# Attention scores from two-part rounded operands, and one reduction for the maxima of two heads

## The chip, the cores and the metric

The kernel runs on one core of a Trainium2 chip. The metric is the device time of one execution in microseconds (us); lower is better. The engines are TensorE (PE for its matmuls, PEld for its weight loads), VectorE (DVE), ScalarE (ACT), GpSimd (POOL) and SyncE (SP, which only issues transfers).

## The reference

Attention over 4 batches, 12 heads, 448 positions and 64 values for each head, then two feed-forward layers of 768 to 2048 to 768 on the 1792 rows that result:

```python
q_n, k_n = rmsnorm(q, g_q), rmsnorm(k, g_k)        # x / sqrt(mean(x*x) + 1e-6) * g
scores = scale * q_n @ k_n.T                       # (448, 448) for each head
attn = exp(scores - scores.max(-1)); attn /= attn.sum(-1) + 1e-9
x = attn @ v                                       # rows of 12 heads * 64 = 768
h = x @ w_in;  x = (s * relu(h)**2 + b) @ w_out    # layer 1
h = x @ w_in2; x = (h * cos(h)) @ w_out2           # layer 2
```

q, k, v and x are float32. The weights come as float64 and are turned to float32 on the chip.

## The kernel before, in words

**Attention.** Two heads make a pair; there are 24 pairs, worked on one after the other, each in four chunks of 112 query rows: 96 chunks `s`, where pair `i = s // 4` and `r = s % 4`. Heads 0 and 1 of a pair lie in partitions 0 to 63 and 64 to 127 of the transposed q and k (`qT`, `kT`), so that their score matmuls use different row halves of TensorE's array. One chunk is `scores(s)` (line 203): two float32 matmuls, one for each head, into two PSUM banks; two reductions on DVE for the maxima (line 222); two exponentials on ACT with the sums beside them (line 230). Two chunks later `turn` (line 240) transposes the exponentials, four transposes for each head into a bank tagged "tp" (two such banks), and copies them out, head 0 by ACT (line 254), head 1 by DVE (line 252). `mix` (line 264) multiplies them with v.

q and k of pair i+1 are made ready during pair i: `flip` (line 186) transposes them on PE at r = 1 (q) and r = 2 (k); `unflip` (line 194) copies the result to SBUF, q by ACT (line 199), k by DVE with the gains multiplied in (line 201). Squares (line 145 on POOL, 147 on ACT) and their sums (line 153, DVE) come three pairs ahead, and `norms` two.

**What sets the order.** The loop at line 313 emits each step. At r = 1 that is: flip q, scores, unflip q, turn; at r = 2: flip k, scores, unflip k, turn, mix. The helper `line` (line 118) ties each attention instruction to the one emitted before it on the same engine: on PE always, on ACT and DVE until 36 chunks (9 pairs, `ALONE`) have been emitted. Within those the engines take the attention's instructions in just the order of the code. Engines work through their queues in order. What isn't tied (the weights' preparation, and after 36 chunks all of ACT's and DVE's work) stands where the program's scheduler put it when the kernel was built. `follow` makes the score matmuls of chunk s wait for the exponentials of chunk s-2.

**Feed-forward.** The first 9 pairs run alone, with some preparation of weights beside them. Then the units of the feed-forward layers are mixed in: `unit_in` (18 matmuls of 448 columns, line 437) and `unit_out` (line 489 in layer 1, 516 in layer 2). Their float32 operands are split into a rounded high part and the low rest (`float32r`, which PE takes in one pass), and each product is three matmuls: high by high, low by high, high by low (`products`, line 100). How many attention steps go between two units is worked out from costs written by hand (0.93 for the scores of a chunk, `PAIR` = 12.1 for a pair). Each half of a weight tile passes ACT (lines 408, 409), DVE (412 to 414), ACT (371) and POOL (374).

Of the kernel before, what the change touches and what calls it, by code (L numbers as in the profile page):

```python
# [10 lines left out]
F32 = mybir.dt.float32  # L11
F32R = mybir.dt.float32r
# [3 lines left out]
ALU = mybir.AluOpType  # L16
# [17 lines left out]
def body(ctx, tc, q, k, v, g_q, g_k, w1_in, w1_out, s_in, b_in, w2_in, w2_out, out):  # L34
# [16 lines left out]
    LAG_T = 2  # L51
    START, GATE = 4, 10
    ALONE = 9
    PAIR = 12.1
    LOOK = 8

    const = ctx.enter_context(tc.tile_pool(name="const", bufs=1))
# [42 lines left out]
    def products(w, x):  # L100
        return ((w[0], x[0]), (w[1], x[0]), (w[0], x[1]))
# [9 lines left out]
    def attention(keep):  # L111
# [6 lines left out]
        def line(engine, first, last=None):  # L118
            if engine in tail and (engine == "PE" or len(exps) <= NCH * ALONE):
                issue_after(first, tail[engine])  # L120
            tail[engine] = last or first
            return first

        def load(i, what):
            b, hp = pairs[i]
            for nm in what:
                src = {"q": q, "k": k, "v": v}[nm]
                t = att.tile([CP, 2, NCH, D], F32, tag=f"raw{nm}", name=f"raw{nm}_{b}_{hp}")
                st[i][nm] = t
                src = src[b, 2 * hp:2 * hp + 2]  # L130
                if i == 0 and nm == "q":
                    t = t.rearrange("p h c d -> p (h c d)").rearrange("p (c h d) -> p c h d", c=NCH, h=2)
                    for j in range(2):
                        nc.sync.dma_start(t[:, :, j, :], src[j].rearrange("(p c) d -> p c d", c=NCH))
                    st[i]["q by chunk"] = t
                else:
                    nc.sync.dma_start(t, src.rearrange("h (p c) d -> p h c d", c=NCH))

        def squares(i):
            b, hp = pairs[i]  # L140
            for nm in "qk":
                t = st[i]["n" + nm] = att.tile([CP, NCH, 2, D], F32, tag=f"n{nm}", name=f"n{nm}_{b}_{hp}")
                t, src = t.rearrange("p c h d -> p (c h d)"), st[i][nm].rearrange("p h c d -> p (h c d)")
                if 1 < i <= ALONE + 2:
                    nc.gpsimd.tensor_tensor(t, src, src, ALU.mult)
                else:
                    line("ACT", nc.scalar.activation(t, src, AF.Square))

        def means(i):
            b, hp = pairs[i]  # L150
            ss = att.tile([CP, 2, 8], F32, tag="ss", name=f"ss_{b}_{hp}")
            for n, nm in enumerate("qk"):
                line("DVE", nc.vector.reduce_sum(ss[:, n, :], st[i]["n" + nm].rearrange("p c h d -> p (c h d)").rearrange("p (a d) -> p a d", d=D), axis=AX.X))  # L153
            tiny = nc.vector if i == 0 else nc.gpsimd
            m = st[i]["m"] = att.tile([CP, 16], F32, tag="m", name=f"m_{b}_{hp}")
            tiny.tensor_scalar(m, ss.rearrange("p a b -> p (a b)"), 1.0 / D, 1e-6, ALU.mult, ALU.add)

        def norms(i):
            b, hp = pairs[i]
            m, tiny = st[i]["m"], nc.vector if i == 0 else nc.gpsimd  # L160
            ln = att.tile([CP, 16], F32, tag="ln", name=f"ln_{b}_{hp}")
            line("ACT", nc.scalar.activation(ln, m, AF.Ln))
            y = att.tile([CP, 16], F32, tag="y", name=f"y_{b}_{hp}")
            line("ACT", nc.scalar.activation(y, ln, AF.Exp, scale=-0.5))
            z = att.tile([CP, 16], F32, tag="z", name=f"z_{b}_{hp}")
            kept = (lambda z: line("DVE", z)) if i == 0 else lambda z: z
            kept(tiny.tensor_tensor(z, y, y, ALU.mult))
            kept(tiny.tensor_tensor(z, z, m, ALU.mult))
            kept(tiny.tensor_scalar(z, z, -0.5, 1.5, ALU.mult, ALU.add))
            kept(tiny.tensor_tensor(y, y, z, ALU.mult))  # L170
            rs = y.rearrange("p (a h c) -> p a h c", a=2, h=2)
            if i == 0:
                st[i]["rs"] = y[:, 0:2 * NCH]
            for n, nm in enumerate("qk"):
                if i == 0 and n == 0:
                    continue
                kept(tiny.tensor_tensor(
                    st[i]["n" + nm].rearrange("p c h d -> p h c d"), st[i][nm],
                    rs[:, n].unsqueeze(3).to_broadcast([CP, 2, NCH, D]), ALU.mult))

        def bank(i, name):
# [12 lines left out]
        def unflip(i, nm):  # L194
            b, hp = pairs[i]
            pt = st[i]["p" + nm]
            t = st[i][nm + "T"] = att.tile([P, S], F32, tag=f"{nm}T", name=f"{nm}T_{b}_{hp}")
            if nm == "q":
                line("ACT", nc.scalar.copy(t, pt))
            else:  # L200
                line("DVE", nc.vector.tensor_scalar(t, pt, gqk, None, ALU.mult))

        def scores(s):
            i, c = divmod(s, NCH)
            key = f"{pairs[i][0]}_{pairs[i][1]}_{c}"
            sc = [ps.tile([P, 512], F32, tag="sc", name=f"sc_{key}_{j}", bufs=4)[:CP, :S] for j in range(2)]
            mm = []
            for j in range(2):
                half = slice(j * D, (j + 1) * D)
                mm.append(nc.tensor.matmul(sc[j], st[i]["qT"][half, c * CP:(c + 1) * CP], st[i]["kT"][half, :], start=True, stop=True))  # L210
            line("PE", *mm)
            issue_after(mm[1], mm[0])
            if s > 1:
                follow(mm[0], exps[s - 2])
            if s == START:
                marks["start"] = mm[1]
            if c == 0:
                st[i]["sums"] = att.tile([CP, NCH, 2], F32, tag="sums", name=f"sums_{key}", bufs=3)
                st[i]["top"] = att.tile([CP, 8], F32, tag="top", name=f"top_{key}", bufs=3)
            tops = [st[i]["top"][:, 2 * c + j:2 * c + j + 1] for j in range(2)]  # L220
            for j in range(2):
                line("DVE", nc.vector.tensor_reduce(tops[j], sc[j], axis=AX.X, op=ALU.max, negate=True))  # L222
            scale = [1.0, 1.0]
            if i == 0:
                both = st[i]["top"][:, 2 * c:2 * c + 2]
                line("DVE", nc.vector.tensor_tensor(both, both, st[i]["rs"][:, 2 * c:2 * c + 2], ALU.mult))
                scale = [st[i]["rs"][:, 2 * c + j:2 * c + j + 1] for j in range(2)]
            for j in range(2):
                pr = st[i]["pr", j, c] = att.tile([CP, S], F32, tag="pr", name=f"pr_{key}_{j}", bufs=8)
                e = line("ACT", nc.scalar.activation(pr, sc[j], AF.Exp, bias=tops[j], scale=scale[j], accum_out=st[i]["sums"][:, c, j:j + 1]))  # L230
            exps.append(e)

# [80 lines left out]
        for s in range(n + 5):  # L313
# [10 lines left out]
                cost += 0.46  # L324
            if s < n:
                scores(s)
                cost += 0.93
            if r == 1:
                emit(unflip, i + 1, "q")
            if r == 2:  # L330
# [96 lines left out]
    def unit_in(layer, seg, ck, f, b):  # L427
# [18 lines left out]
        if layer == 0:  # L446
            r = ma.tile([P, S], F32, tag="t0", name=f"r_{key}")
            nc.scalar.activation(r, h, AF.Relu)
            r2 = ma.tile([P, S], F32, tag="t1", name=f"r2_{key}")
            nc.gpsimd.tensor_tensor(r2, r, r, ALU.mult)  # L450
            gt = ma.tile([P, S], F32, tag="t2", name=f"gt_{key}")
            nc.vector.tensor_scalar(gt, r2, sb[:, 0:1], sb[:, 1:2], ALU.mult, ALU.add)  # L452
        else:
            hs = ma.tile([P, S], F32, tag="t0", name=f"hs_{key}")
            nc.scalar.copy(hs, h)
            h = hs
            kk = ma.tile([P, S], F32, tag="t1", name=f"kk_{key}")
# [229 lines left out]
```

## Time and profile before

| | us |
|---|---|
| three timed runs | 1299.21, 1291.16, 1298.42 |
| median of the runs | 1298.42 |
| the profiled execution | 1293.51 |
| its span, first to last instruction | 1291.4 |

The granted TensorE clock of the profiled execution was 0.996 of full speed. In the rows below, a duration is that of one instruction from its start to its end, and neighbours on an engine overlap at the ends; how long an instruction keeps its engine is read from the start of the next one. In a timeline, "x4" stands for four instructions merged in one row, and the number in brackets is idle time before the row with what ended it.

### The profile page before, as it was taken

To read this page: it belongs to the slowest core of one execution; us is meant where nothing else is said; L and a number is where in the kernel's file an instruction comes from. 1 tells how busy PE (TensorE), PEld (TensorE's weight loads), DVE (VectorE), ACT (ScalarE), POOL (GpSimd) and SP (SyncE) were. 2 spreads that over 40 slices of the span, in tenths; PEclk is the share of its full clock that TensorE was granted. 3 is DMA by queue.
4 is the path that set the end of the run, shared out by engine and by line. 5 is a ranking of instruction groups with operands and counts; after the bars stand their busy time and mean duration, and the time that the engine had idled before them with its cause. 6 is when DMAs were issued, how large, how long until landed. Compare 5 with 4: busy or idle time off the path is not lost.

```text
span 1291.4 us, 18598 instructions
## 1 busy us (share of the span) xinstructions
PE 1246.4 (97%) x6624; PEld 1034.9 (80%) x6624; DVE 857.9 (66%) x1456; ACT 744.8 (58%) x1674; POOL 581.5 (45%) x643
## 2 busy tenths in 40 slices
PE   5999998999999999989999999999999999999998
PEld 2555675677677767779999999999999999999998
DVE  5898768876868767654454456854767767677655
ACT  4787767755666555525332225787656656566640
POOL 3665646454553524414333233565444445354531
PEclk9999999999999999999999999999999999999999
DMA  3333324543344223353222112111212111111105
GB/s 97 108 99 120 99 90 126 159 127 102 123 133 126 100 89 94 106 165 104 78 71 69 55 56 74 51 49 51 71 50 74 50 50 49 49 50 50 62 1 171
DMA packets 82222, 111.32 MB, mean 86 GB/s; under 512 B 8113, under 2 KB 72145, under 8 KB 82129
## 3 DMA queue, kind: packets, MB, share of 16 engines
q1 hardware_dynamic: 82128, 110.13, 27.8%
q8 instruction: 52, 0.85, 0.3%
q14 instruction: 42, 0.34, 0.1%
HBM read 86.51 MB, written 23.59 MB: 85 GB/s over the span
## 4 chain that ended last, share of the span: by engine, by line
PE 58%; DVE 18%; ACT 14%; POOL 4%; issue 3%; DMA 3%; SPq 0%; DVEq 0%; ACTq 0%; POOLq 0%
PE ph L437 24%; PE po L516 14%; PE po L489 13%; ACT pr L230 4%; DVE t L413 3%; DVE t L414 3%; DVE top L222 2%; PE sc L210 2%; PE av L271 2%; PE tp L248 2%; DVE c L412 2%; DVE gt L461 2%; DVE ss L153 1%; DVE gt L462 1%; ACT pT L254 1%
## 5 line engine op out<-in xcount | busy, mean ns | idle before, releaser
L437 PE MATMUL ph<-xh,wl 128*128 128x448 f32 x768 | 283.4, 369 | 0.0
L437 PE MATMUL ph<-xl,wh 128*128 128x448 f32 x768 | 281.6, 367 | 0.0
L437 PE MATMUL ph<-xh,wh 128*128 128x448 f32 x768 | 280.0, 369 | 0.0
L467 POOL TENSOR_TENSOR gl<-gt,gh 128x448 fp32r<-128x448 f32 x128 | 157.0, 1231 | 185.0 <-ACT gh L466 184.9
L374 POOL TENSOR_TENSOR wl<-t,wh 128x384 fp32r<-128x384 f32 x128 | 139.1, 1102 | 71.7 <-ACT wh L371 70.7
L437 PEld LDWEIGHTS ph<-xh,wh 128*128 128x128 f32 x768 | 144.1, 188 | 16.5 <-issue 2.0
L489 PE MATMUL po<-gh,wh 128*128 128x448 f32 x384 | 145.9, 382 | 11.2 <-DVE acc L498 10.6
L498 DVE TENSOR_TENSOR acc<-po,acc 128x448 f32<-128x448 f32 x168 | 103.2, 619 | 80.3 <-PE po L489 80.1
L230 ACT ACTIVATE pr<-sc,top 112x448 f32<-112x448 f32 x184 | 116.4, 635 | 67.1 <-DVE top L222 66.9
L371 ACT CAST wh<-t 128x384 fp32r<-128x384 f32 x200 | 95.4, 513 | 103.4 <-PE po L489 53.3
L516 PE MATMUL po<-wh,gh 128*128 128x384 f32 x448 | 152.1, 340 | 2.3 <-ACT acc L522 1.1
L437 PEld LDWEIGHTS ph<-xh,wl 128*128 128x128 f32 x768 | 144.3, 188 | 12.1 <-issue 2.0
L437 PEld LDWEIGHTS ph<-xl,wh 128*128 128x128 f32 x768 | 144.3, 188 | 12.1 <-issue 1.3
L516 PE MATMUL po<-wl,gh 128*128 128x384 f32 x448 | 149.8, 335 | 0.4 <-POOL wl L374 0.4
L516 PE MATMUL po<-wh,gl 128*128 128x384 f32 x448 | 149.8, 334 | 0.0
L524 DVE TENSOR_TENSOR acc<-po,acc 128x384 f32<-128x384 f32 x196 | 105.4, 551 | 60.3 <-PE po L516 60.2
L489 PE MATMUL po<-gl,wh 128*128 128x448 f32 x384 | 142.2, 371 | 0.0
L489 PE MATMUL po<-gh,wl 128*128 128x448 f32 x384 | 142.1, 370 | 0.0
L465 POOL TENSOR_TENSOR gt<-hs,gt 128x448 f32<-128x448 f32 x64 | 78.3, 1223 | 129.0 <-ACT gt L464 118.7
L222 DVE TENSOR_REDUCE top<-sc 112x1 f32<-112x448 f32 x192 | 112.9, 616 | 23.2 <-PE sc L210 22.9
L466 ACT CAST gh<-gt 128x448 fp32r<-128x448 f32 x128 | 71.3, 564 | 97.9 <-DVE gt L452 59.6
L248 PEld LDWEIGHTS tp<-ident,pr 112*112 112x112 f32 x768 | 78.6, 133 | 60.5 <-issue 12.5
(89 smaller groups left out, 2258.4 us busy)
## 6 DMA issues: line engine op xcount, KB each, us to landing
raw<-in_moe_w_in_dram SPq DMA_DIRECT2D x64, 384.0 KB, 3.4
raw<-in_moe_w_out_dram SPq DMA_DIRECT2D x64, 384.0 KB, 3.2
t<-wd SPq DMA_DIRECT2D x72, 192.0 KB, 2.4
wd<-t SPq DMA_DIRECT2D x64, 192.0 KB, 3.1
rawk<-in_k_dram SPq DMA_DIRECT2D x24, 224.0 KB, 3.5
rawv<-in_v_dram SPq DMA_DIRECT2D x24, 224.0 KB, 3.0
rawq<-in_q_dram SPq DMA_DIRECT2D x23, 224.0 KB, 3.1
xd<-xf SPq DMA_DIRECT2D x12, 224.0 KB, 3.9
```

Source lines behind the costliest of these rows:

```text
L222: line("DVE", nc.vector.tensor_reduce(tops[j], sc[j], axis=AX.X, op=ALU.max, negate=True))
L230: e = line("ACT", nc.scalar.activation(pr, sc[j], AF.Exp, bias=tops[j], scale=scale[j], accum_out=st[i]["sums"][:, c, j:j + 1]))
L248: mm = [nc.tensor.transpose(tp[:, kc * CP:(kc + 1) * CP], pr[:, kc * CP:(kc + 1) * CP], ident[:CP, :CP]) for kc in range(NCH)]
L371: z = nc.scalar.copy(wh, w)
L374: eng.tensor_tensor(wl, w, wh.bitcast(F32), ALU.subtract)
L437: nc.tensor.matmul(h, a, m, start=(c == 0 and n == 0), stop=(c == NE - 1 and n == 2))
L465: nc.gpsimd.tensor_tensor(gt, h, gt, ALU.mult)
L467: nc.gpsimd.tensor_tensor(gl, gt, gh.bitcast(F32), ALU.subtract)
L489: marks["out"] = nc.tensor.matmul(po, a, m, start=(f == 0 and n == 0), stop=(f == CF - 1 and n == 2))
L498: nc.vector.tensor_tensor(at, po, at, ALU.add)
L516: nc.tensor.matmul(po, a, m, start=(f == 0 and n == 0), stop=(f == CF - 1 and n == 2))
L524: nc.vector.tensor_tensor(at, po, at, ALU.add)
```

## The change

The score operands are split as in the feed-forward layers, and each chunk's two matmuls become six, head by head in turn, into one tile of two banks. The two maxima of a chunk come from one reduction over both banks. q and k of a pair lie in one tile, so that their squares and sums are one instruction each (two for pair 0). To find room, the exponentials get 7 buffers in place of 8, and layer 1's squared activation is written in place while attention runs. The hand-written costs follow.

```diff
-    PAIR = 12.1
+    PAIR = 11.0
...
         def unflip(i, nm):
             pt = st[i]["p" + nm]
-            t = st[i][nm + "T"] = att.tile([P, S], F32, tag=f"{nm}T", name=f"{nm}T_{b}_{hp}")
+            hi, lo = (att.tile([P, S], F32R, tag=f"{nm}{z}", name=f"{nm}{z}_{b}_{hp}") for z in "hl")
+            st[i][nm + "T"] = hi, lo
             if nm == "q":
-                line("ACT", nc.scalar.copy(t, pt))
+                line("ACT", nc.scalar.copy(hi, pt))
+                line("DVE", nc.vector.tensor_tensor(lo, pt, hi.bitcast(F32), ALU.subtract))
             else:
-                line("DVE", nc.vector.tensor_scalar(t, pt, gqk, None, ALU.mult))
+                line("ACT", nc.scalar.activation(hi, pt, AF.Copy, scale=gqk))
+                line("DVE", nc.vector.scalar_tensor_tensor(lo, pt, gqk, hi.bitcast(F32), ALU.mult, ALU.subtract))
 
         def scores(s):
-            sc = [ps.tile([P, 512], F32, tag="sc", name=f"sc_{key}_{j}", bufs=4)[:CP, :S] for j in range(2)]
+            both = ps.tile([P, 2, 512], F32, tag="sc", name=f"sc_{key}", bufs=2)[:CP, :, :S]
+            sc = [both[:, j, :] for j in range(2)]
             mm = []
-            for j in range(2):
-                half = slice(j * D, (j + 1) * D)
-                mm.append(nc.tensor.matmul(sc[j], st[i]["qT"][half, c * CP:(c + 1) * CP], st[i]["kT"][half, :], start=True, stop=True))
+            for n, (x, y) in enumerate(products(st[i]["qT"], st[i]["kT"])):
+                for j in range(2):
+                    half = slice(j * D, (j + 1) * D)
+                    mm.append(nc.tensor.matmul(sc[j], x[half, c * CP:(c + 1) * CP], y[half, :], start=(n == 0), stop=(n == 2)))
...
-            for j in range(2):
-                line("DVE", nc.vector.tensor_reduce(tops[j], sc[j], axis=AX.X, op=ALU.max, negate=True))
+            line("DVE", nc.vector.tensor_reduce(st[i]["top"][:, 2 * c:2 * c + 2], both, axis=AX.X, op=ALU.max, negate=True))
...
-                cost += 0.93
+                cost += 0.65
...
-            r2 = ma.tile([P, S], F32, tag="t1", name=f"r2_{key}")
+            r2 = pools["mb"].tile([P, S], F32, tag="t1", name=f"r2_{key}") if "mb" in pools else r
```

## Rows read from the trace of the kernel before

**Rows 1.** The page: busy time, share of the span and instructions of each engine.

```profile
PE 1246.4 (97%) x6624; PEld 1034.9 (80%) x6624; DVE 857.9 (66%) x1456; ACT 744.8 (58%) x1674; POOL 581.5 (45%) x643
```

**Rows 2.** Busy by stretch: length; PE, PEld, DVE, ACT, POOL; clock; DMA share; GB/s.

```profile
50.00:100.00 50.00, 48.88 (x313) 25.73 (x311) 44.88 (x82) 39.38 (x112) 31.67 (x52) 1.00 0.34 105
100.00:140.00 40.00, 38.91 (x244) 19.75 (x242) 35.49 (x66) 32.63 (x93) 23.73 (x42) 1.00 0.38 121
140.00:525.00 385.00, 369.82 (x2016) 268.78 (x2016) 279.27 (x489) 241.15 (x590) 182.38 (x223) 0.99 0.36 113
```

**Rows 3.** The chain of waits, 95 to 125 us: shares by line; start, us, what.

```profile
by line: ACT pr L230 29.9%; DVE top L222 12.8%; ACT pT L254 11.4%; DVE c L412 11.3%; DVE ss L153 7.9%; DVE t L413 5.6%; ACT c L408 4.7%; ACT qT L199 4.2%; DVE pT L252 3.5%; DVE t L414 3.1%; ACT xh L96 3.0%; issue 0.8%; ACT ln L162 0.8%; ACT
...
94.96 0.42 ACT qT L199
...
98.01 1.13 DVE c L412
...
99.22 0.56 DVE t L413
...
101.84 1.19 DVE ss L153 x2
...
103.64 1.34 ACT pr L230 x4
...
107.31 0.42 ACT qT L199
...
119.67 0.42 ACT qT L199
```

**Rows 4.** Timeline of PE, three places alone and one at 411 us.

```profile
104.17 1.01 PE L210 MATMUL sc<-kT,qT 64*112 64x448 f32 x4
105.11 0.98 PE L248 MATMUL tp<-ident,pr 112*112 112x112 f32 x8
...
108.75 1.72 PE L271 MATMUL av<-pT,rawv 112*64 112x448 f32 x8
...
411.81 3.23 PE L271 MATMUL av<-pT,rawv 112*64 112x448 f32 x16
```

**Rows 5.** The chain of waits, later: 36 rounded matmuls of 448 columns.

```profile
618.96 7.30 PE ph L437 x36
```

**Rows 6.** Timeline of weight loads (PEld) at the scores of one chunk.

```profile
404.29 0.28 PEld L210 LDWEIGHTS sc<-kT,qT 64*112 64x112 f32 x4
```

**Rows 7.** Groups by line: reductions, 140 to 525 us and the whole span.

```profile
L222 DVE TENSOR_REDUCE top<-sc 112x1 f32<-112x448 f32 x110 | 64.9, 614 | 8.1 <-PE sc L210 7.8
...
L153 DVE TENSOR_REDUCE ss<-nk 112x8 f32<-112x512 f32 x24 | 16.3, 677 | 0.9 <-ACT nk L147 0.9
```

**Rows 8.** Timeline of DVE, 104 to 110 us (r = 0, 1, 2).

```profile
104.05 0.61 DVE L252 COPY pT<-tp 112x448 f32<-112x448 f32 x1
104.58 0.61 DVE L279 TENSOR_TENSOR xf<-av,xf 128x448 f32<-128x448 f32 x1
...
105.22 1.14 DVE L222 TENSOR_REDUCE top<-sc 112x1 f32<-112x448 f32 x2
106.28 0.61 DVE L252 COPY pT<-tp 112x448 f32<-112x448 f32 x1
107.45 1.16 DVE L222 TENSOR_REDUCE top<-sc 112x1 f32<-112x448 f32 x2 [0.55 <-PE sc L210]
108.52 0.68 DVE L201 TENSOR_SCALAR kT<-pt_k,gqk 128x448 f32<-128x448 f32 x1
109.11 0.61 DVE L252 COPY pT<-tp 112x448 f32<-112x448 f32 x1
```

**Rows 9.** Timeline of ACT, 105 to 108 us (r = 1).

```profile
105.98 0.63 ACT L230 ACTIVATE pr<-sc,top 112x448 f32<-112x448 f32 x1
...
107.19 0.54 ACT L199 COPY qT<-pt_q 128x448 f32<-128x448 f32 x1
107.61 0.57 ACT L254 COPY pT<-tp 112x448 f32<-112x448 f32 x1
```

More of the change, by code (lines that the diff above doesn't have):

```diff
@@ L125, in load @@
             b, hp = pairs[i]
[L126 to L131, printed above, removed]
+            if what == "v":
+                t = st[i]["v"] = att.tile([CP, 2, NCH, D], F32, tag="rawv", name=f"rawv_{b}_{hp}")
+                nc.sync.dma_start(t, v[b, 2 * hp:2 * hp + 2].rearrange("h (p c) d -> p h c d", c=NCH))
+                return
+            st[i]["qk"] = att.tile([CP, 2, 2, NCH, D], F32, tag="rawqk", name=f"rawqk_{b}_{hp}")
+            for n, src in enumerate((q, k)):
+                t, src = st[i]["qk"][:, n], src[b, 2 * hp:2 * hp + 2]
+                if i == 0 and n == 0:
                     t = t.rearrange("p h c d -> p (h c d)").rearrange("p (c h d) -> p c h d", c=NCH, h=2)
@@ L140, in squares @@
             b, hp = pairs[i]
[L141 to L147, printed above, removed]
+            t = att.tile([CP, 2, NCH, 2, D], F32, tag="nqk", name=f"nqk_{b}_{hp}")
+            st[i]["nq"], st[i]["nk"] = t[:, 0], t[:, 1]
+            t = st[i]["n"] = t.rearrange("p a c h d -> p (a c h d)")
+            src = st[i]["qk"].rearrange("p a h c d -> p (a h c d)")
+            if i == 0:
+                half = NCH * 2 * D
+                for z in (slice(0, half), slice(half, 2 * half)):
+                    line("ACT", nc.scalar.activation(t[:, z], src[:, z], AF.Square))
+            elif 1 < i <= ALONE + 2:
+                nc.gpsimd.tensor_tensor(t, src, src, ALU.mult)
+            else:
+                line("ACT", nc.scalar.activation(t, src, AF.Square))
         def means(i):
             b, hp = pairs[i]
-            ss = att.tile([CP, 2, 8], F32, tag="ss", name=f"ss_{b}_{hp}")
-            for n, nm in enumerate("qk"):
-                line("DVE", nc.vector.reduce_sum(ss[:, n, :], st[i]["n" + nm].rearrange("p c h d -> p (c h d)").rearrange("p (a d) -> p a d", d=D), axis=AX.X))
+            ss = att.tile([CP, 16], F32, tag="ss", name=f"ss_{b}_{hp}")
+            for z in (range(2) if i == 0 else [0]):
+                w = 8 if i == 0 else 16
+                line("DVE", nc.vector.reduce_sum(ss[:, z * 8:z * 8 + w], st[i]["n"][:, z * 8 * D:(z * 8 + w) * D].rearrange("p (a d) -> p a d", d=D), axis=AX.X))
             tiny = nc.vector if i == 0 else nc.gpsimd
             m = st[i]["m"] = att.tile([CP, 16], F32, tag="m", name=f"m_{b}_{hp}")
-            tiny.tensor_scalar(m, ss.rearrange("p a b -> p (a b)"), 1.0 / D, 1e-6, ALU.mult, ALU.add)
+            tiny.tensor_scalar(m, ss, 1.0 / D, 1e-6, ALU.mult, ALU.add)
         def norms(i):
@@ L177, in norms @@
                 kept(tiny.tensor_tensor(
-                    st[i]["n" + nm].rearrange("p c h d -> p h c d"), st[i][nm],
+                    st[i]["n" + nm].rearrange("p c h d -> p h c d"), st[i]["qk"][:, n],
                     rs[:, n].unsqueeze(3).to_broadcast([CP, 2, NCH, D]), ALU.mult))
@@ L205, in scores @@
             key = f"{pairs[i][0]}_{pairs[i][1]}_{c}"
-            sc = [ps.tile([P, 512], F32, tag="sc", name=f"sc_{key}_{j}", bufs=4)[:CP, :S] for j in range(2)]
+            both = ps.tile([P, 2, 512], F32, tag="sc", name=f"sc_{key}", bufs=2)[:CP, :, :S]
+            sc = [both[:, j, :] for j in range(2)]
             mm = []
-            for j in range(2):
-                half = slice(j * D, (j + 1) * D)
-                mm.append(nc.tensor.matmul(sc[j], st[i]["qT"][half, c * CP:(c + 1) * CP], st[i]["kT"][half, :], start=True, stop=True))
-            line("PE", *mm)
-            issue_after(mm[1], mm[0])
+            for n, (x, y) in enumerate(products(st[i]["qT"], st[i]["kT"])):
+                for j in range(2):
+                    half = slice(j * D, (j + 1) * D)
+                    mm.append(nc.tensor.matmul(sc[j], x[half, c * CP:(c + 1) * CP], y[half, :], start=(n == 0), stop=(n == 2)))
+            line("PE", mm[0], mm[-1])
+            for x, y in zip(mm, mm[1:]):
+                issue_after(y, x)
             if s > 1:
@@ L215, in scores @@
             if s == START:
-                marks["start"] = mm[1]
+                marks["start"] = mm[-1]
             if c == 0:
@@ L228, in scores @@
             for j in range(2):
-                pr = st[i]["pr", j, c] = att.tile([CP, S], F32, tag="pr", name=f"pr_{key}_{j}", bufs=8)
+                pr = st[i]["pr", j, c] = att.tile([CP, S], F32, tag="pr", name=f"pr_{key}_{j}", bufs=7)
                 e = line("ACT", nc.scalar.activation(pr, sc[j], AF.Exp, bias=tops[j], scale=scale[j], accum_out=st[i]["sums"][:, c, j:j + 1]))
@@ L456, in unit_in @@
             h = hs
-            kk = ma.tile([P, S], F32, tag="t1", name=f"kk_{key}")
+            kk = pools["mb"].tile([P, S], F32, tag="t1", name=f"kk_{key}")
             nc.scalar.activation(kk, h, AF.Copy, scale=1.0 / (2 * math.pi), bias=MAGIC)
```

## The prediction

> **What bounds the kernel now.** I read the shares of the engines first, then busy time by stretch, then the chain of waits inside a stretch, because the first view misleads here. By it PE is busy 97% of the span, DVE 66%, ACT 58% [rows 1], as if every PE microsecond saved were a microsecond won. The stretches show two regimes [rows 2]. From 140 to 525 us, attention mixed with feed-forward units, PE is busy 370 of 385 us and DVE only 279: PE binds. From 50 to 140 us, attention alone, PE is busy 88 of 90 us but DVE 80 and ACT 72, and busy PE time includes the pipeline's tail of each matmul, so it doesn't say who sets the pace. The chain of waits does: from 95 to 125 us its listed shares hold no PE at all, only ACT and DVE handing over to each other [rows 3]. The same ACT copy stands in it at 94.96, 107.31 and 119.67 us, so one pair takes 12.35 us there. All three engines are near their limit in this stretch, and what the change adds on DVE and ACT must be walked through in their own order.
>
> **PE, per chunk.** Now the scores take 105.11 - 104.17 = 0.94 us from their first matmul to the next work. The row holds four passes of 448 columns (two for each float32 matmul), all within 1.01 us, so the heads run side by side, two by two [rows 4]. What one float32 pass of 448 columns costs in a run comes from the mixing matmuls: 16 against 8 of them, also two side by side, differ by (3.23 - 1.72) / 4 = 0.378 us a pass [rows 4]. Two passes are 0.755, and the remaining 0.185 is entering and leaving the half-row arrangement. After the change there are three rounds of rounded matmuls. A rounded matmul of 448 columns takes 7.30 / 36 = 0.203 us on the full array [rows 5]. If two of them share the array as the float32 ones do, a chunk costs 3 x 0.203 + 0.185 = 0.79 us: 0.14 to 0.15 saved. The ends: 0.189 a round, half a float32 pass, saves 0.19; six in a row, 6 x 0.203 + 0.185 = 1.40, cost 0.46. I take 0.14, since the float32 pairs run side by side in the same place.
>
> The weights of the new rounds have to be loaded too. The trace has all four loads of a chunk within 0.28 us of the start of its 1.01 us of matmuls, so the second pass's weights arrive while the first still runs [rows 6]. The Trainium skill ("TensorE: Matmul & The Clock Gate", part 3, on what overlaps) says that a weight load goes beside running matmuls only when its row group differs, though an earlier sentence of that part also allows the array's background weights. By the narrow rule each of the two further rounds would show its load; the trace goes against it, and it is a rival below.
>
> Of the 96 chunks, 110 / 2 = 55 have their maxima after 140 us [rows 7], where PE binds: 55 x 0.14 = 7.7 us won.
>
> **DVE and ACT, instruction by instruction.** Reductions: 448 elements take 614 ns, 512 take 677 [rows 7], so 1.0 ns an element more, and 896 in one should take 1.05 us and hold DVE about 1.0, against 1.07 for two (107.45 to 108.52) [rows 8]. That saves 0.07 us of DVE a chunk, but the first exponential now waits 1.05 instead of 0.61 us. The merged sums of squares save about 0.1 us a pair. The key's copy leaves DVE (108.52 to 109.11, 0.59) and becomes a copy on ACT, 0.42 as for q [rows 8, 9]. Two subtractions come to DVE for each pair. The nearest form, PSUM and SBUF into SBUF, is the row of xf: 0.61 long, some 0.53 of DVE [rows 8]; I take 0.6 for each, with 0.53 and 0.9 as ends. Sum: DVE gains 1.2 - 0.6 - 0.3 - 0.1 = +0.2 us a pair, ACT +0.4. As busy time this is little.
>
> **The new wait.** The order is what costs. Now at r = 1 DVE does its reductions at 105.22 and at 106.28 copies the transposed exponentials out, waiting for nothing from ACT; q's copy sits on ACT behind both exponentials of that chunk (105.98 to 107.19, the copy done at 107.73) [rows 8, 9]. After the change the subtraction stands on DVE between reduction and copy, and it reads the high part, which ACT makes behind those two exponentials. So DVE stands still from the end of its reduction until two exponentials (1.21) and a copy (0.54) are done: 1.8 us with the handovers. Queued behind the subtraction are the copy of transposed exponentials, for which PE's next transposes wait (two banks), and the next reduction, for which ACT waits. At r = 2 the same happens with k, whose DVE copy needed nothing from ACT before. In the first 36 chunks the code ties this order, so the scheduler can't go around it.
>
> A pair alone, on DVE: four reductions 4.0, four copies 2.1, xf and reciprocal 0.64 (104.58 to 105.22) [rows 8], sums of squares 1.1, two subtractions 1.2, and the weights' three steps, from 98.01 to 99.22 for the first [rows 3], about 2.2 together. That is 11.2, and two waits of 1.8 make 14.8 us, against 12.35 now. If the weights' steps, which are not tied, all fell into the waits, 12.6 us would be left. I take 14.3: in the rows they stand between the second wait and the fourth reduction, where only part can slide. So +1.95 us for each of the 8 pairs that follow the first in the tied order: +15.6. PE's saving there (4 x 0.14 a pair) is idle time. The first pair starts one handover later (ACT's copy, then the subtraction) and is as tied: +1. The ends for a pair: -0.6 (PE sets the pace after all, 4 x 0.14) and +2.8 (nothing fills, and ACT's added copy of 0.4 comes in full), so -5 to +22 for eight.
>
> **Mixed stretch.** There ACT and DVE have room (241 and 279 of 385 us) [rows 2] and the order is the scheduler's, but the banks of the turned q and k are held until the subtraction. I add 2 us (0 to 5) for this against the 7.7.
>
> **At nothing:** the exponentials' 7 buffers (their transposes are issued on PE ahead of the scores that come next) and the activation squared in place; a layer-1 unit comes every 18 x 0.203 = 3.7 us at the soonest [rows 5] and there are two buffers. The merged loads and squares come pairs ahead. Without that cover each would cost a fraction of a microsecond a pair.
>
> **Sum.** 1293.5 + 15.6 + 1 - 7.7 + 2 = 1304.4, against the profiled execution's 1293.5. That one lies below the median of the runs (1298.4); the four executions have a mean of 1295.6, 2 us above it, so I give 1306.
>
> **Rivals.**
> 1. *PE sets the pace everywhere*, because DVE's waits fall into its idle time (10 of 90 us now [rows 2]) and the weights' steps fill the rest: 96 x 0.14 = 13.4 saved, about 1281. For it: PE's 97%. Against: two waits of 1.8 us a pair are more than the 1.3 us a pair that DVE idles now, and the chain without PE.
> 2. *The weights' steps fill the waits but no more*: 12.6 us a pair, +2 for eight, then 1 - 7.7 + 2: about 1291. For it: they aren't tied. Against: their place now.
> 3. *Weights of each round exposed*: 0.28 us for four loads is 0.07 each; two further rounds cost 0.14, and the chunk saves nothing. Then only the wait is left: 1293.5 + 15.6 + 1 + 2 = 1312. Against: rows 6. The narrow rule of the Trainium skill quoted above would bring this about.
> 4. *The heads run one after the other*, so that the change doesn't do what it says: 0.46 x 55 = +25 where PE binds, +20 alone, about 1339. Against: the float32 passes.
>
> The forecast and rivals 3 and 4 end slower; rivals 1 and 2 are those that don't. They decide at one point: whether a pair alone stays under about 13 us.
>
> **How the numbers follow.** Forecast 0.50 (its own range 1297 to 1316), rival 1 0.18, rival 2 0.14, rival 3 0.10, rival 4 0.08. A measurement of this kernel tells about 1%, 13 us, from no change. Faster by that (below 1285) is most of rival 1: 0.15. Slower (above 1311) is a quarter of the forecast, most of rival 3 and rival 4: 0.32. The rest, 0.53, lies between. The range 1280 to 1322 holds rival 1, the forecast and rival 3, and leaves out little but rival 4.
>
> **What would show it.** In the profile after: six rounded matmuls of a chunk within about 0.85 us, the next work 0.79 after the first (1.40 if the heads don't share; 0.94 if weights show). Alone, pairs 14 to 15 us apart, DVE idle before the subtractions with ACT's high part as the releaser, some 1.8 us each, and PE waiting at the transposes. The first feed-forward matmul comes some 16 us later; from there to the attention's end the stretch is some 6 us shorter, and the rest is as long as before. The prediction is wrong if pairs alone keep to 12.4 us or less, or if the mixed stretch grows.

## The result and the profile after

The changed kernel took 1305.61 us (median of 7 runs, 1302.06 to 1307.86), the kernel before 1292.33 us on the same chip (7 runs): a ratio of 1.009, 95% interval 1.0064 to 1.0117. The forecast was 1306. The total came out right, but in part because errors in its terms cancelled; the experiments take it apart.

The page of the kernel after, busy time of each engine (beside [rows 1]):

```profile
PE 1239.0 (95%) x6816; PEld 1053.7 (81%) x6816; DVE 852.6 (65%) x1361; ACT 756.1 (58%) x1685; POOL 589.4 (45%) x633
```

DVE is busy 5 us less than before and ACT 11 more, and ACT is idle for 42% of the span, so the busy sums don't say where 13 us come from. The time by place does. The first feed-forward matmul (start of the first and of the last one at the end of "x768", of before and of after in two fences) tells the stretch of attention alone from the rest:

```profile
L437 PE MATMUL ph<-xh,wh x768: 358/368/472, 140.8 to 1254.6; 128*128 128x448 f32 x192
```

```profile
L450 PE MATMUL ph<-xh,wh x768: 358/368/473, 162.3 to 1267.1; 128*128 128x448 f32 x192
```

Attention alone grew by 162.3 - 140.8 = 21.5 us. What follows it, in the two profiled spans, went from 1291.4 - 140.8 = 1150.6 to 1303.8 - 162.3 = 1141.5: 9 us shorter. With the medians in place of the spans, as in the table further down, it is 7.6.

The matmuls with v tell where attention ends (start of the first and of the last one; before, then after):

```profile
L271 PE MATMUL av<-pT,rawv x384: 539/539/591, 34.6 to 546.0; 112*64 112x448 f32 x192
```

```profile
L284 PE MATMUL av<-pT,rawv x384: 539/539/1006, 42.0 to 558.5; 112*64 112x448 f32 x192
```

The mixed stretch takes 546.0 - 140.8 = 405.2 us before and 558.5 - 162.3 = 396.2 after, and what follows it 745.4 and 745.3. So all of the 9 us lie in the mixed stretch, where the prediction looked for them.

Busy time by stretch of the kernel after (columns as in [rows 2]):

```profile
32.00:40.00 8.00, 7.02 (x34) 5.25 (x34) 4.58 (x7) 5.54 (x17) 6.37 (x14) 0.50 0.53 159
50.00:100.00 50.00, 41.64 (x290) 24.49 (x290) 35.83 (x56) 35.87 (x102) 31.21 (x43) 0.98 0.28 80
100.00:140.00 40.00, 34.75 (x240) 19.81 (x240) 29.27 (x45) 29.41 (x82) 23.42 (x31) 0.98 0.33 97
```

From 50 to 140 us PE was busy 88 of 90 us before and is busy 76 now; DVE went from 80 to 65 and ACT from 72 to 65. All three idle more, as engines do that wait for each other in turn. Who waits for whom, 50 to 160 us (engine and line, what it waited for, us in total, times, longest):

```profile
ACT pr L243 <- DVE top L235: 24.2, 22, 1.8
...
DVE ql L209 <- ACT qh L208: 14.3, 7, 2.0
DVE kl L212 <- ACT kh L211: 13.5, 7, 1.9
PE tp L261 <- ACT pT L267: 12.9, 20, 1.0
```

DVE stands before its two subtractions 14.3 / 7 = 2.04 and 13.5 / 7 = 1.93 us a pair. One of them, in the timeline of DVE after (beside [rows 8]; start, us, what, and in brackets the idle time before it):

```profile
109.39 1.04 DVE L235 TENSOR_REDUCE top<-sc 112x2 f32<-112x896 f32 x1
112.46 0.62 DVE L209 TENSOR_TENSOR ql<-pt_q,qh 128x448 fp32r<-128x448 f32 x1 [2.04 <-ACT qh L208]
113.00 0.61 DVE L265 COPY pT<-tp 112x448 f32<-112x448 f32 x1
113.53 1.08 DVE L235 TENSOR_REDUCE top<-sc 112x2 f32<-112x896 f32 x1
```

and in the timeline of ACT after (beside [rows 9]):

```profile
110.67 0.63 ACT L243 ACTIVATE pr<-sc,top 112x448 f32<-112x448 f32 x1
...
111.28 0.64 ACT L243 ACTIVATE pr<-sc,top 112x448 f32<-112x448 f32 x1
...
111.88 0.54 ACT L208 CAST qh<-pt_q 128x448 fp32r<-128x448 f32 x1
112.30 0.57 ACT L267 COPY pT<-tp 112x448 f32<-112x448 f32 x1
```

The two rows of exponentials and the one of the cast are what DVE waits through: its reduction ends at 110.43, the cast at 112.42, the subtraction starts at 112.46. The copy and the reduction behind it are queued, and ACT's next exponentials wait for that reduction.

PE's part, in the timelines of matmuls (first fence, beside [rows 4]) and of weight loads (second, beside [rows 6]) of one chunk after:

```profile
106.06 0.46 PE L223 MATMUL sc<-kh,qh 64*112 64x448 f32 x2
106.36 0.36 PE L223 MATMUL sc<-kh,ql 64*112 64x448 f32 x2
106.56 0.37 PE L223 MATMUL sc<-kl,qh 64*112 64x448 f32 x2
106.86 0.98 PE L261 MATMUL tp<-ident,pr 112*112 112x112 f32 x8
```

```profile
106.06 0.17 PEld L223 LDWEIGHTS sc<-kh,qh 64*112 64x112 f32 x2 [0.70 <-issue]
106.16 0.18 PEld L223 LDWEIGHTS sc<-kh,ql 64*112 64x112 f32 x2
106.36 0.17 PEld L223 LDWEIGHTS sc<-kl,qh 64*112 64x112 f32 x2
```

The chunk takes 106.86 - 106.06 = 0.80 us. Rounds two and three follow 0.30 and 0.20 us after the one before, two heads side by side, and each one's weights are loaded while the round before runs (106.16 and 106.36).

Pairs alone, by the first score matmul of each: 12.35 us before, 14.08 to 14.86 after from the third pair to the tenth, 14.44 in the mean. The first two pairs take longer. The first matmul of the first and of the third pair, before and then after:

```profile
11.28 1.84 PE L210 MATMUL sc<-kT,qT 64*112 64x448 f32 x4 [0.87 <-DVE kT L201]
...
40.18 1.01 PE L210 MATMUL sc<-kT,qT 64*112 64x448 f32 x4
```

```profile
13.50 0.71 PE L223 MATMUL sc<-kh,qh 64*112 64x448 f32 x2 [0.72 <-ACT kh L211]
...
29.01 0.60 PE L261 MATMUL tp<-ident,pr 112*112 112x112 f32 x4 [3.97 <-ACT pT L267]
...
48.22 0.46 PE L223 MATMUL sc<-kh,qh 64*112 64x448 f32 x2
```

The first pair starts 2.2 us later, and from the first to the third it is 28.90 us before and 34.72 after: another 5.8 us. Within it PE waits 3.97 us in one piece for ACT's copy of transposed exponentials, and then its granted clock is 0.50 of full speed, the 1.2 GHz level, from 32 to 40 us.

### The profile page after: what moved, and what is told of

Its sections match the earlier page's. It is cut to its first block, busy times and chain, and to the rows that moved or that the text cites. A ratio compares the mean times of both kernels' runs of the same rounds, so it can differ in the third digit from the quotient of the medians.

```text
span 1303.8 us, 18879 instructions
## 1 busy us (share of the span) xinstructions
PE 1239.0 (95%) x6816; PEld 1053.7 (81%) x6816; DVE 852.6 (65%) x1361; ACT 756.1 (58%) x1685; POOL 589.4 (45%) x633
## 4 chain that ended last, share of the span: by engine, by line
PE 58%; DVE 10%; ACT 6%; DMA 2%; issue 2%; POOL 1%; DVEq 0%; ACTq 0%; POOLq 0%
PE ph L450 25%; PE po L529 14%; PE po L502 13%; PE av L284 2%; DVE t L426 2%; PE tp L261 2%; DVE gt L474 2%; PE sc L223 2%; DVE gt L475 2%; DVE t L427 1%; DMA xr<-xd 1%; DMA raw<-in_moe_w_in_dram 1%; DVE top L235 1%; ACT gt L476 1%; DVE c L425 1%
## 5 line engine op out<-in xcount | busy, mean ns | idle before, releaser
L480 POOL TENSOR_TENSOR gl<-gt,gh 128x448 fp32r<-128x448 f32 x128 | 154.3, 1210 | 178.4 <-ACT gh L479 178.3
L502 PE MATMUL po<-gl,wh 128*128 128x448 f32 x384 | 140.8, 367 | 0.0
L261 PE MATMUL tp<-ident,pr 112*112 112x112 f32 x768 | 108.7, 270 | 27.0 <-ACT pT L267 17.7
```

Source lines behind the costliest of these rows:

```text
L261: mm = [nc.tensor.transpose(tp[:, kc * CP:(kc + 1) * CP], pr[:, kc * CP:(kc + 1) * CP], ident[:CP, :CP]) for kc in range(NCH)]
L480: nc.gpsimd.tensor_tensor(gl, gt, gh.bitcast(F32), ALU.subtract)
L502: marks["out"] = nc.tensor.matmul(po, a, m, start=(f == 0 and n == 0), stop=(f == CF - 1 and n == 2))
```

## The experiments

One table first; each run is taken up below. "Alone" is the usual (median) period of a pair in attention alone, "first" the start of the first feed-forward matmul, both from the run's trace; "rest" is the median minus "first"; "clock" is the mean granted clock over all runs of the kernel. Each ratio is to runs of the kernel before that were made beside it; 1291.7 is its median in the two largest groups of these (24 and 23 runs). "Rest" scatters as the medians do: the intervals of the ratios reach 1.6 to 4.7 us to either side.

| kernel | median us (runs) | ratio to before, 95% | alone | first | rest | clock |
|---|---|---|---|---|---|---|
| before | 1291.7 | 1 | 12.35 | 140.8 | 1150.9 | 0.997 |
| after | 1305.6 (7) | 1.009 (1.0064 to 1.0117) | 14.45 | 162.3 | 1143.3 | 0.992 |
| two maxima | 1308.8 (4) | 1.0123 (1.0096 to 1.015) | 14.64 | 164.6 | 1144.2 | 0.989 |
| no wait on high | 1303.2 (4) | 1.0084 (1.0058 to 1.011) | 14.45 | 161.6 | 1141.6 | 0.992 |
| split before scores | 1315.3 (5) | 1.0177 (1.0153 to 1.0201) | 16.0 | 171.3 | 1144.0 | 0.985 |
| two products | 1304.4 (4) | 1.0098 (1.0062 to 1.0135) | 14.3 | 161.2 | 1143.2 | 0.983 |
| high on DVE | 1295.8 (8) | 1.0045 (1.0024 to 1.0066) | 13.18 | 148.0 | 1147.8 | 0.993 |
| banks apart | 1300.8 (4) | 1.0074 (1.0059 to 1.0089) | 13.58 | 155.0 | 1145.8 | 0.992 |
| before, merged | 1288.3 (9) | 0.9973 (0.9957 to 0.9988) | 12.84 | 143.8 | 1144.5 | 0.997 |
| DVE, banks apart | 1292.4 (11) | 1.0013 (1.0001 to 1.0025) | 12.24 | 141.5 | 1150.9 | 0.993 |
| split, late merge | 1285.8 (12) | 0.9963 (0.9945 to 0.998) | 12.24 | 142.0 | 1143.8 | 0.994 |
| float32, late merge | 1286.2 (6) | 0.9961 (0.9946 to 0.9976) | 12.35 | 140.1 | 1146.1 | 0.997 |
| split, banks apart | 1286.8 (12) | 0.9961 (0.9947 to 0.9975) | 12.24 | 140.2 | 1146.6 | 0.995 |

The theory under test, W in the expectations: in the tied order, the handover from ACT's high part to DVE's subtraction sets the pair. Its rivals: A, the added work itself does; M, the merged reduction does.

**Two maxima.** A reduction for each head again, on the tile that both heads share.

```diff
-            line("DVE", nc.vector.tensor_reduce(st[i]["top"][:, 2 * c:2 * c + 2], both, axis=AX.X, op=ALU.max, negate=True))
+            for j in range(2):
+                line("DVE", nc.vector.tensor_reduce(tops[j], sc[j], axis=AX.X, op=ALU.max, negate=True))
```

> The maxima of the two heads come from two reductions again, everything else is the changed kernel. Theory W (a pair alone is long because each subtraction on VectorE waits for ScalarE's high part, which stands behind two exponentials): the first exponential starts about 0.43 us earlier in each of the two waits, the waits themselves stay; a pair alone goes from 14.45 to about 13.8 us, the whole to about 1300. Rival M (the merged reduction is what costs): a pair alone falls to 12.3 to 12.8 us and the whole to about 1287. Rival A (the added work on ScalarE and VectorE costs): a pair stays at 14.4 or is 0.1 longer, the whole stays at 1305.

It gave nothing: 14.64 us a pair, nearest to what rival A expected, and not W. The timelines of DVE and of ACT in this run say why (two fences):

```profile
113.70 1.14 DVE L236 TENSOR_REDUCE top<-sc 112x1 f32<-112x448 f32 x2
```

```profile
114.88 0.63 ACT L244 ACTIVATE pr<-sc,top 112x448 f32<-112x448 f32 x1 [1.85 <-DVE top L236]
```

The pair of reductions runs from 113.70 to 114.84, and the first exponential begins only then, 0.6 us after its own maximum is there. The heads share a tile, so the exponential waits for both reductions. This run doesn't price the merging; "banks apart" below does.

**No wait on high.** Both subtractions subtract the previous pair's high part, so the low parts are not the reference's.

```diff
+            other = st[i - 1][nm + "T"][0] if i else hi
...
-                line("DVE", nc.vector.tensor_tensor(lo, pt, hi.bitcast(F32), ALU.subtract))
+                line("DVE", nc.vector.tensor_tensor(lo, pt, other.bitcast(F32), ALU.subtract))
...
```

> The subtraction takes as its second operand the high part of the pair before, which has long been there, in place of its own pair's: the same work on every engine, without the wait for ScalarE; the low parts are not those of the reference. Theory W: a pair alone falls from 14.45 to about 12.5 us (12.2 to 12.9), the first feed-forward matmul comes back from 162 to 143 to 146 us, and the whole is about 1287. Rival M: a pair alone stays above 13.8, the whole above 1300. Rival A: no change, 14.4 and 1305.

A miss: 14.45 us, as after and as rival A expected. In the timelines of DVE and ACT the subtraction still stands behind the cast whose result it no longer reads:

```profile
97.39 0.62 DVE L210 TENSOR_TENSOR ql<-pt_q,qh 128x448 fp32r<-128x448 f32 x1 [2.04 <-ACT qh L209]
```

```profile
96.82 0.55 ACT L209 CAST qh<-pt_q 128x448 fp32r<-128x448 f32 x1
```

Cast and subtraction read the same PSUM tile, pt_q. The cast ends at 97.37, the subtraction starts at 97.39, with the same 2.04 us of idle time before it. So the wait isn't for the data of the high part alone; that the shared tile orders the two is inferred. The Trainium skill ("PSUM — Partial Sum Buffer", section on bank collisions) says that the compiler's scheduler adds a dependency between instructions of different engines that touch the same 32 partitions of one bank, reads as well as writes, ACT against DVE included; this trace, with its 2.04 us, agrees with such an order. In "two maxima" the order reached further: there the exponential waited for a reduction over the other bank of its tile. The run therefore left W untested.

**Split before scores.** The turned q and k are split before a round's score work instead of behind it.

```diff
-            if s < n:
-                scores(s)
-                cost += 0.65
             if r == 1:
...
                 emit(unflip, i + 1, "k")
+            if s < n:
+                scores(s)
+                cost += 0.65
```

> The high and low parts of the next pair are emitted ahead of the chunk's scores instead of behind them, so that the high part's copy stands on ScalarE before the two exponentials; all work is done. Theory W: VectorE waits only for transposes and one copy, some 0.5 us before its reduction; a pair alone takes 12.3 to 13.0 us, the whole is 1284 to 1290, faster than the kernel before by 0.2 to 0.7 per cent. Rivals M and A: a pair alone stays at 14 or more, the whole above 1300.

A miss, in the wrong direction: 16.0 us a pair in the mean (15.0 to 17.0), above 14 as rivals A and M expected. The chain of waits of this run (start, us, what):

```profile
114.26 0.43 ACT qh L208
...
114.71 0.62 DVE ql L209
115.34 1.01 DVE top L235
...
116.37 1.34 ACT pr L243 x4
```

Every row ends within 0.02 us of the next one's start, ACT and DVE in turn, and k's split does the same from 118.13 us on: the wait has only moved ahead of the reduction, and the subtraction now delays the exponentials too. The place of the wait changes the pair by 1.5 us with the same work in it, which speaks for W against A.

**Two products.** The third product of the scores is left out.

```diff
-            for n, (x, y) in enumerate(products(st[i]["qT"], st[i]["kT"])):
+            for n, (x, y) in enumerate(products(st[i]["qT"], st[i]["kT"])[:2]):
...
-                    mm.append(nc.tensor.matmul(sc[j], x[half, c * CP:(c + 1) * CP], y[half, :], start=(n == 0), stop=(n == 2)))
+                    mm.append(nc.tensor.matmul(sc[j], x[half, c * CP:(c + 1) * CP], y[half, :], start=(n == 0), stop=(n == 1)))
```

> The third product (high of k by low of q or the like) is left out, so each chunk has two rounds of matmuls in place of three: 0.20 us of TensorE less a chunk. Theory: TensorE binds only where feed-forward units are mixed in, 55 chunks, so 55 x 0.2 = 11 us less there and nothing alone, where a pair stays at 14.4 us: the whole about 1295. Rival P (TensorE sets the pace everywhere): 96 x 0.2 = 19 us less, a pair alone 0.8 us shorter, the whole about 1286.

Alone nothing changes (14.3), so PE is not what sets the pair. But the rest stays at 1143.2, so the expected 11 us didn't come, though the interval of this run is wide (4.7 us to either side). Busy time by stretch in this run, and then the same stretch after, point to where they may have gone:

```profile
220.00:260.00 40.00, 34.37 (x166) 22.84 (x167) 33.53 (x44) 27.98 (x70) 23.88 (x30) 0.83 0.43 131
260.00:280.00 20.00, 18.39 (x100) 15.24 (x99) 17.55 (x31) 14.07 (x33) 6.52 (x7) 0.91 0.55 174
```

```profile
220.00:260.00 40.00, 33.68 (x190) 23.99 (x190) 35.12 (x49) 29.67 (x72) 27.63 (x32) 0.96 0.45 135
260.00:280.00 20.00, 17.69 (x105) 14.13 (x104) 16.74 (x29) 15.13 (x37) 3.85 (x7) 1.00 0.52 167
```

PE has fewer matmuls there (166 against 190; a third of the score matmuls is gone) at a lower granted clock (0.83 against 0.96, 0.91 against 1.00): 0.13 x 40 + 0.09 x 20 = 7 us of full speed less. Over all runs the mean clock is 0.983 against 0.992, 0.009 x 1304 = 12 us of full speed, about what the leaner chunk should have won, though part of that lies in the stretch alone (from 50 to 140 us the clock is 0.94 here and 0.98 after). That the saving turned into idle time and a lower clock fits these rows; no run held the clock fixed, so it isn't shown as the only cause.

**High on DVE.** DVE makes the high part too, so nothing is handed over.

```diff
-                line("ACT", nc.scalar.copy(hi, pt))
+                line("DVE", nc.vector.tensor_copy(hi, pt))
...
-                line("ACT", nc.scalar.activation(hi, pt, AF.Copy, scale=gqk))
+                line("DVE", nc.vector.tensor_scalar(hi, pt, gqk, None, ALU.mult))
```

> The high parts of q and k are made on VectorE, right ahead of the subtraction, in place of ScalarE, so that no VectorE instruction of the split stands behind ScalarE's exponentials (the run with another second operand kept the wait: the subtraction still began only after ScalarE had read the same PSUM bank). VectorE gets two copies of 0.55 us a pair more, ScalarE 0.85 less. Theory W (the handover to ScalarE and back inside VectorE's tied order): VectorE's own work of some 12.4 us a pair then sets the pace, a pair alone takes 12.5 to 13.2 us, the whole is 1288 to 1294. Rival M (the merged reduction): a pair alone stays at 14 or more, the whole above 1300. Rival A (added work): VectorE has more to do, a pair alone is 15 or more.

**Banks apart.** A tile and a reduction for each head, the split as in the change.

```diff
-            both = ps.tile([P, 2, 512], F32, tag="sc", name=f"sc_{key}", bufs=2)[:CP, :, :S]
-            sc = [both[:, j, :] for j in range(2)]
+            sc = [ps.tile([P, 512], F32, tag="sc", name=f"sc_{key}_{j}", bufs=4)[:CP, :S] for j in range(2)]
...
-            line("DVE", nc.vector.tensor_reduce(st[i]["top"][:, 2 * c:2 * c + 2], both, axis=AX.X, op=ALU.max, negate=True))
+            for j in range(2):
+                line("DVE", nc.vector.tensor_reduce(tops[j], sc[j], axis=AX.X, op=ALU.max, negate=True))
```

> Each head's scores have a tile of their own again and their own reduction, so that the first exponential can start after the first reduction, as before the change (in the run with two reductions on one tile it still began after the second); the split and its wait stay. Theory W: two of the handovers are 0.45 us shorter, a pair alone about 13.5 us (13.2 to 13.9), the whole about 1298. Rival M: a pair alone 12.3 to 12.8, the whole 1284 to 1288.

**Before, merged.** The kernel before with only the shared tile and the one reduction.

```diff
+            both = ps.tile([P, 2, 512], F32, tag="sc", name=f"sc_{key}", bufs=2)[:CP, :, :S]
+            sc = [both[:, j, :] for j in range(2)]
...
+            line("DVE", nc.vector.tensor_reduce(st[i]["top"][:, 2 * c:2 * c + 2], both, axis=AX.X, op=ALU.max, negate=True))
```

> The kernel before with one part of the change alone: both heads' scores in one tile and one reduction for the two maxima; float32 products and unsplit q and k as before. Theory W: the exponentials start 0.45 us later where ScalarE waits for them, one or two times a pair; a pair alone 12.6 to 13.2 us in place of 12.35, the whole 1294 to 1299. Rival M: a pair alone 14 or more and the whole 1306 or more.

**DVE, banks apart.** "High on DVE" and "banks apart" together; of their diffs:

```diff
+                line("DVE", nc.vector.tensor_copy(hi, pt))
...
+                line("DVE", nc.vector.tensor_scalar(hi, pt, gqk, None, ALU.mult))
...
+                line("DVE", nc.vector.tensor_reduce(tops[j], sc[j], axis=AX.X, op=ALU.max, negate=True))
```

> High parts on VectorE and a tile and reduction for each head. Theory W: neither handover is left longer than before the change; VectorE has some 12.6 us of work a pair, a pair alone takes 12.5 to 13.0, the whole 1285 to 1291, a little faster than the kernel before. If VectorE's work as such set the pace more tightly, a pair would take 13.5 and the whole 1296.

The first score matmul of two neighbouring pairs, in the timelines of PE: high on DVE, banks apart, and DVE with banks apart.

```profile
93.59 0.46 PE L223 MATMUL sc<-kh,qh 64*112 64x448 f32 x2
...
106.77 0.46 PE L223 MATMUL sc<-kh,qh 64*112 64x448 f32 x2
```

```profile
87.19 0.46 PE L222 MATMUL sc<-kh,qh 64*112 64x448 f32 x2
...
100.78 0.46 PE L222 MATMUL sc<-kh,qh 64*112 64x448 f32 x2
```

```profile
90.81 0.46 PE L222 MATMUL sc<-kh,qh 64*112 64x448 f32 x2
...
103.06 0.46 PE L222 MATMUL sc<-kh,qh 64*112 64x448 f32 x2
```

They are 13.18, 13.59 and 12.25 us; before, merged has 12.84. Alone, this settles W against A. With the split on DVE and the banks apart, DVE has the most work of all these kernels (two high parts and two subtractions a pair, 0.6 to 0.7 us each, for the one copy of before) and the pair is 0.11 us shorter than before. DVE is then busy nearly all the time (columns as in [rows 2]):

```profile
50.00:100.00 50.00, 47.26 (x346) 28.32 (x342) 49.72 (x91) 39.28 (x111) 37.36 (x50) 1.00 0.34 104
```

From there to the change there are two steps, and each has about the same price whichever is taken first. High parts on ACT cost 13.58 - 12.24 = 1.34 with the banks apart and 14.45 - 13.18 = 1.27 merged. Merging costs 14.45 - 13.58 = 0.87 with the handover and 13.18 - 12.24 = 0.94 without it. So the handover makes about 1.3 of the 2.1 us, and rival M is right for the other 0.9 or so. Where the handover stands, part of merging's price shows in DVE's waits. In the timeline of DVE with the banks apart they are 1.44 and 1.40 us, against 2.04 and 1.93 in the change:

```profile
106.91 0.62 DVE L209 TENSOR_TENSOR ql<-pt_q,qh 128x448 fp32r<-128x448 f32 x1 [1.44 <-ACT qh L208]
...
110.53 0.69 DVE L212 SCALAR_TENSOR_TENSOR kl<-pt_k,gqk,kh 128x448 fp32r<-128x448 f32 x1 [1.40 <-ACT kh L211]
```

With float32 scores merging costs only 12.84 - 12.35 = 0.49; why it is dearer with the split is not shown.

The first two pairs show the handover more strongly still. In "high on DVE" the third pair starts at 41.84 us, 1.7 later than before and 6.4 earlier than in the change, and the clock from 32 to 40 us is 1.00 (timeline of PE, busy time by stretch):

```profile
41.84 0.46 PE L223 MATMUL sc<-kh,qh 64*112 64x448 f32 x2
```

```profile
32.00:40.00 8.00, 7.39 (x58) 4.61 (x56) 6.80 (x11) 5.08 (x17) 5.57 (x9) 1.00 0.53 172
```

The pairs came within W's ranges or just under (12.24 for 12.5 to 13.0), but the whole missed W's forecasts in all four runs, by 1.4 to 5.7 us: W says nothing of the mixed stretch.

The rest tells another story. Merged float32 scores have 1144.5 there, 6.4 below before, while the three-product scores with the high parts on DVE and banks apart have 1150.9: nothing won. So three kernels were made that keep the cheap order alone and differ after it.

**Split, late merge.** High parts on DVE and banks apart for the first nine pairs (high parts for ten), from there as in the change; the pool of the score banks is switched at the 36th chunk.

```diff
-                line("DVE", nc.vector.tensor_copy(hi, pt))
+                line("DVE", nc.vector.tensor_copy(hi, pt)) if i <= ALONE else line("ACT", nc.scalar.copy(hi, pt))
...
+            if s == NCH * ALONE:
+                sc_scope.close()
+                pools["sc"] = att_scope.enter_context(tc.tile_pool(name="sc2", bufs=2, space=PSUM))
```

> The changed kernel with two repairs for the stretch in which attention runs alone: there the high parts are made on VectorE and each head has its own bank and reduction; from the tenth pair on everything is as in the change. Theory S (what the stretch with feed-forward units gained by the change is its own: less TensorE work and one reduction fewer): the first feed-forward matmul comes at 141 to 142 us, and the rest is as long as in the change, 1305.6 - 162.3 = 1143; the whole about 1285. Rival T (the rest was short only because weights had been prepared during the longer first stretch): the rest grows to 1150 again, the whole about 1292.

**Float32, late merge.** The kernel before with the merged reduction from the tenth pair on and no split at all.

```diff
+            if s < NCH * ALONE:
+                for j in range(2):
+                    line("DVE", nc.vector.tensor_reduce(tops[j], sc[j], axis=AX.X, op=ALU.max, negate=True))
+            else:
+                line("DVE", nc.vector.tensor_reduce(st[i]["top"][:, 2 * c:2 * c + 2], pair, axis=AX.X, op=ALU.max, negate=True))
```

> The kernel before with one reduction over two banks from the tenth pair on, nothing else: no split, float32 products. With merging everywhere the rest after the first feed-forward matmul was 1288.3 - 143.8 = 1144.5 us, against 1150.9 before. Theory S: the merged reduction helps the stretch with feed-forward units by itself; first such matmul at 141, the whole about 1285.5. Rival T: the whole 1291.

**Split, banks apart.** "DVE, banks apart" with the high parts on ACT after the tenth pair.

```diff
-                line("DVE", nc.vector.tensor_scalar(hi, pt, gqk, None, ALU.mult))
+                line("DVE", nc.vector.tensor_scalar(hi, pt, gqk, None, ALU.mult)) if i <= ALONE else line("ACT", nc.scalar.activation(hi, pt, AF.Copy, scale=gqk))
```

> As the run with the high parts on VectorE and banks apart, but from the tenth pair on the high parts are ScalarE's, as in the change. That run's rest was 1292.4 - 141.5 = 1151 us. If VectorE's two further copies a pair were what ate TensorE's saving there, the rest is 1146 here and the whole 1287; if it was the reductions that weren't merged, the rest stays at 1150 and the whole at 1291.

The first feed-forward matmul of the three, in the order of their sections:

```profile
L462 PE MATMUL ph<-xh,wh x768: 358/368/740, 142.0 to 1248.6; 128*128 128x448 f32 x192
```

```profile
L449 PE MATMUL ph<-xh,wh x768: 358/368/473, 140.1 to 1247.2; 128*128 128x448 f32 x192
```

```profile
L450 PE MATMUL ph<-xh,wh x768: 358/368/474, 140.2 to 1246.1; 128*128 128x448 f32 x192
```

All three begin it as early as the kernel before, within 1.2 us, and all three are faster than before by 0.4%, each interval below 1. They came as expected: as theory S has it in the first two, as the first of the two cases in the third.

Against 1150.9, the rest is shorter by 7.1 us with both parts, by 4.8 with merged reductions alone, by 4.3 with three products alone (high parts on ACT). These differ by little more than their scatter of about 2 us, and in the three profiled spans (1285.3, 1283.9 and 1282.9 us) the rest is 1143.3, 1143.8 and 1142.7, against 1150.6: shorter by 7.3, 6.8 and 7.9. So either part wins 4 to 8 us there, and no run shows that both win more than one. With the high parts left on DVE the gain of three products is gone (1150.9): in the mixed stretch the two copies are better on ACT, alone they are better on DVE. These three are the fastest kernels of this case, at 1286 us, and one of them has no split at all: no run shows the split to win anything beyond late merging alone.

## Why the prediction came out right, and where not

- **The new wait** is there, and is the larger part. 1.8 us were predicted before each subtraction, 2.04 and 1.93 came; +1.95 us a pair was predicted, +2.09 came from the third to the tenth pair. But taking the handover away gives back only 1.27 to 1.34 of it; the rest is the merged reduction's, so that these two agree so well is partly luck. "Only part can slide" held: 14.8 were worked out with nothing filling the waits, 14.3 taken, 14.44 measured.
- **The merged reduction** was mis-sized: "saves 0.07 us of DVE a chunk, but the first exponential now waits 1.05 instead of 0.61". The wait was named and not added up; it entered the sum only as the point where DVE's wait begins. It measured 0.49 us a pair with float32 scores and 0.87 to 0.94 with the split. In the mixed stretch merging wins 4.8 to 6.4 us by the medians, which the prediction didn't have at all.
- **The first pair**, "+1", was the term that failed by most. The first pair starts 2.2 us later and the next two periods lose 5.8: 8.0 us by the third pair's start, where the prediction has +1 for the first and +1.95 for each of the next. The clock at 0.50 from 32 to 40 us lies in it. Some 6.4 of the 8.0 go with the handover: in "high on DVE" the third pair starts at 41.84 us and the clock holds. What share of them is the clock's is not shown. With seven more pairs at 2.09 it makes 22.6, and so the first feed-forward matmul came 21.5 us later, not "some 16".
- **The mixed stretch** had nearly the right size and the wrong reason. "Where PE binds: 55 x 0.14 = 7.7 us won" less 2 was to make 5.7; 7.6 came. But merged reductions alone, with PE's chunk unchanged, win 4.8, as much within the scatter as three products without merging (4.3); and a further 0.2 us of PE work a chunk, taken away, brings nothing near its 11 us. PE's busy share of 370 in 385 us was read as "PE binds". The runs show that PE's saving isn't simply won there; whether it goes into waits for DVE and ACT or into the lower clock stays open.
- **PE's chunk** was right: 0.79 predicted, 0.80 measured, 0.94 before. That ends rivals 3 and 4: the heads run side by side, and the weights of each round are hidden (loads at 106.16 and 106.36 beside matmuls of the same two row halves). It goes against the narrow rule of the Trainium skill ("TensorE: Matmul & The Clock Gate", part 3) weighed in the prediction.
- **Rivals 1 and 2** end with the pairs at 14.45 us. PE doesn't set the pace alone (two products leaves them at 14.3). Rival 1's time is 1293.5 - 13.4 = 1280, not 1281; nothing hangs on it.
- **The base**: the forecast stood on 1295.6 for the kernel before, which came in 3 us lower (1292.3). The rise was 13.3 us, not 10.9, so the closeness of 1306 to 1305.6 is partly luck: 5 us too little at the start, 2 too little won later, 3 too much in the base.

## What to carry to other kernels

Where two engines work in a tied order, walk the handovers one by one before adding up busy time: the same split cost 1.3 us a pair on ACT and DVE together and nothing on DVE alone, although DVE was the busier engine. Choose the engine of a step by stretch, not by the average; here that was DVE in attention alone and ACT in the mixed stretch, and of the kernels with the split only those two that mix them so beat the kernel before. And measure the parts of a change one by one and by stretch: a total that agrees can hide errors that cancel, and a part that goes unpriced (here the merged reduction, late) can hold the whole gain.

## What the runs showed that was not expected

- A subtraction on DVE began only after ACT's read of the same PSUM tile although it no longer used its result: 2.04 us of idle time with and without the data dependence. Splitting the reduction didn't release the first exponential either (0.6 us late) while both heads shared one tile.
- The mean granted clock tends to be lower where PE idles more. By the pages PE is idle 45 us of the span before (clock 0.997), 65 after (0.992) and 72 with two products (0.983); "split before scores", with 64 and 0.985, shows that the sum of idle time isn't all of it, and which brings about which is not shown. With work taken from PE where it doesn't quite bind, the clock was 0.83 of full speed for 40 us, where the change has 0.96.
